# Four passes over a KV cache on one core: an even background in the last pass, weight rows on ScalarE's DMA queue, the last Wq columns transposed ahead, full PSUM units

## The chip, the core and the metric

The kernel runs as one program on one core of a Trainium2 chip. The metric is the device time of one execution in microseconds (us): the median of three runs. A hardware profile of one more execution gives the rows that are read here. The engines of the core are called TensorE (PE; its weight loads are shown apart as PEld), VectorE (DVE), ScalarE (ACT), GpSimd (POOL) and SyncE (SP); each takes its own instructions in a fixed order and waits for the others on semaphores. Sixteen DMA engines move data between device memory (HBM) and the on-chip memory (SBUF); matmuls write to PSUM.

## What is computed

One step of decoding through two equal blocks, forward and backward. Each block is attention over a cache of 65,536 positions and then a dense layer; both blocks use the same cache and the same weights:

```python
x = x + A_ref(layernorm(x), k_cache, v_cache, wq, wo)   # 32 query heads, 4 KV groups, Dh = 128
x = x + B_ref(layernorm(x), w1, b1, w2, b2)             # h = relu(ln(x) @ w1 + b1)**2 ; h @ w2 + b2
x = x + A_ref(layernorm(x), k_cache, v_cache, wq, wo)
x = x + B_ref(layernorm(x), w1, b1, w2, b2)
_out, _vjp = jax.vjp(f, x, k_cache, v_cache, wq, wo, w1, b1, w2, b2)
_grads = _vjp(grad_out)
```

One token is decoded (x is 1 x 1024, bf16), so everything is a matrix-vector product, except the gradients of the weights and of the cache, which are outer products. K and V hold 67 MB each, their gradients as much again; Wq and Wo 8.4 MB each, w1 and w2 7.3 MB each, and their gradients as much again.

## The kernel before, in words

The cache is walked four times: forward of the first block's attention (pass 1), forward of the second's (pass 2), backward of the second's (pass 3), and pass 4, which does the backward of the first's and writes the gradients of K and V for both blocks. Between the passes lie dense parts (the products with w1 and w2). The four KV groups are done one after the other. A pass is cut into **items** of 8 columns, a column being 128 positions; a group has 512 columns, so 64 items, and a pass 256. `pipeline` (L455) calls its stages item by item with a lag for each stage, and runs what stands in `bg` for that item behind them; `at` (L468) puts a task there.

**Slabs.** K and V come in slabs of 1 MB, 32 columns, four items. `Ring.slot` (L215) gives the slot that was used longest ago, and `slab` (L248) starts the transfer on SP's queue. SP takes its transfers in order: one that waits for a free slot or row buffer holds all behind it. In pass 4 the ring has the five areas 0 to 4, and area 12 until shortly before the second group; `group_done` (L1146) adds two slots after the second group and one after the third.

**Pass 4** (`attn_bwd4`, L791). Per item: `vT` transposes 8 columns of V on TensorE (L836) and `evac` (L143; ScalarE's line is L153, VectorE's L156) copies them out of PSUM; `vS` multiplies them with the gradient of the output (L855) into one PSUM tile `ps_dp`, of which there is one buffer; a matmul with `sel2` (L851) starts each such tile. When a **unit** of 24 columns is full (the last of a group has 8), VectorE multiplies it with the two blocks' exps (L864, L865) into X, GpSimd copies the exps beside them (L866, L867), and TensorE transposes X (L872). Six items behind `vT`, `k8` accumulates the gradient of the queries (L893) and forms the outer products for the gradients of K and V (L899), which VectorE and ScalarE evict as 128x1024 pieces into a staging area; after 32 columns GpSimd starts the two 1 MB writes (L906, L907). At the end of a group `dqT` is formed (L909). The unit of passes 1 to 3 is 56 columns of 64 places (`UB`, L63), the last 8.

**The background of pass 4.** `OutGrad.later` (L671) forms the output gradient of the three later groups: each of 24 rows of Wo (256 KB) is fetched into one of two buffers (L677, on SP's queue) and multiplied with a vector broadcast to all partitions, on VectorE (L381), and summed by ScalarE (L382). `outer2` (L927) makes the weights' gradients in units of 1024 output columns: two matmuls (L949), an eviction, and after two units or so a write (L953). `rows_into` (L916) lays the vectors out as rows for it: 128-column transposes (L924) and copies of 2x512 on VectorE (L925). `QueryGrad.early` (L701) multiplies rows of Wq with dqT of the first three groups, as dots on VectorE and ScalarE. Due times are written by hand (L1129 to L1144): the units for w2, w1 and Wo from item 72 to item 202, then, from item 202 to 248, the 24 dots with Wq, one an item, and the units for Wq.

**The end.** After the last group, `rows_into` for the last part of Wq's gradient, `QueryGrad.last` (L718: two slabs of Wq, a broadcast of dqT, eight row dots by `RowDots`, L385), eight units of `outer2`, the backward of the layer norm (L322) and the write of the gradient of x (L293).

**The end of pass 2.** V lags K by 76 items. When K is through, `fetch_w1` (L997) loads the eight rows of w1 for the dense part that follows into areas 6 to 13, while V goes on. Areas 10 and 11 hold the scores of the last group, from which the exps are formed (L586), areas 12 and 13 those of the group before.

The order of the instructions on each engine is not the order of these calls: the framework puts each instruction as early as its own estimate of the dependencies allows. In the built program the 24 fetches of Wo rows stand among SP's first 17 slabs of pass 4, six of them in a row, though the tasks are due over the first 170 items.

Of the kernel before, what the change touches and what calls it, by code (L numbers as in the profile page):

```python
# [18 lines left out]
def kernel(  # L19
# [42 lines left out]
    SLOTS = 512 // R  # L62
    UB = SLOTS - 8  # L63
# [3 lines left out]
    SL4 = 512 // R2  # L67
    UB4 = SL4 - 8
# [448 lines left out]
    def attn_fwd(L, order, eT, s_areas, more=None, keep=(), have=()):  # L517
# [26 lines left out]
        def kS(idx):  # L544
            g, c8 = kit[idx]
            if c8 == 0:
                state["S"] = s_areas[order.index(g) % 2].bitcast(F32).rearrange("p (r c) -> p r c", c=C)
                state["pm"] = tmp.tile([P, R, (C + UB - 1) // UB], F32, name="pm_all")
            S_sb, pm_all = state["S"], state["pm"]
            kt = state.pop(("kt", idx))  # L550
            for i in range(8):
                c = c8 + i
                slot = c % UB
                if slot == 0:
                    state["ps_s"] = ps_sc([P, SLOTS, R])
                ps_s = state["ps_s"]
                nc.tensor.matmul(ps_s[:, slot:slot + 8, :].rearrange("p a b -> p (a b)"), lhsT=kt[:, i, :],  # L557
                                 rhs=L["qpad"][:, g, :, :].rearrange("p a b -> p (a b)"), start=True, stop=True)
                if slot == UB - 1 or c == C - 1:
# [73 lines left out]
    class OutGrad:  # L633
# [37 lines left out]
        def later(self, vbc, g, bg, i0, step, rows=None, lead=None):  # L671
# [3 lines left out]
            def fetch(k):  # L675
                box[k] = rows.next()
                nc.sync.dma_start(out=box[k], in_=A_wo[g * GD + k * P:g * GD + (k + 1) * P, :])  # L677
# [16 lines left out]
    class QueryGrad:  # L694


        def __init__(self, dqT, lname):
            self.dqT, self.lname = dqT, lname
            self.y = vec.tile([P, DC, G], F32, name=lname + "_dny")

        def early(self, gs, bg, i0, step, vbc_area):  # L701
# [7 lines left out]
            def one(kc, i):  # L709
                if i == 0:  # L710
                    box["v"] = slab(w_rows(A_wq, kc * P, 1, gs[0] * GD, len(gs) * GD), 1, len(gs) * GD)
                dot_va(box["v"][:, 0, i * GD:(i + 1) * GD], box["vbc"][:, i * GD:(i + 1) * GD], self.y[:, kc, i:i + 1], GD)
            at(bg, i0, start)
            for kc in range(DC):
                for i in range(len(gs)):
                    at(bg, i0 + 1 + (kc * len(gs) + i) * step, lambda kc=kc, i=i: one(kc, i))

        def last(self, g, vbc_area):  # L718
            y = row_dots(A_wq, 0, DC, g * GD, GD, self.dqT[:, g * R:(g + 1) * R], self.lname + "_dnl", vbc_area)
            nc.vector.tensor_copy(out=self.y[:, :, G - 1], in_=y)  # L720
            dn = vec.tile([P, DC], F32, name=self.lname + "_dn")
# [3 lines left out]
    def attn_bwd3(L, og, order, eT, dqT, bg):  # L725
# [20 lines left out]
        def vS(idx):  # L746
            g, c8 = kit[idx]
            if c8 == 0:
                nc.vector.tensor_copy(out=dOpad[:, g, 0, :], in_=og.dOT[:, g * R:(g + 1) * R])
                nc.vector.tensor_copy(out=ndt[:, :, :], in_=og.nd2[:, g * R:(g + 1) * R].unsqueeze(1).to_broadcast([64, SLOTS, R]))  # L750
            vt = state.pop(("vt", idx))
            for i in range(8):
                c = c8 + i
                slot = c % UB
                if slot == 0:
                    state["ps_dp"] = ps_sc([P, SLOTS, R])
# [3 lines left out]
                last = (slot == UB - 1 or c == C - 1)  # L760
                nc.tensor.matmul(ps_dp[:, slot:slot + 8, :].rearrange("p a b -> p (a b)"), lhsT=vt[:, i, :],  # L761
                                 rhs=dOpad[:, g, :, :].rearrange("p a b -> p (a b)"), start=False, stop=last)
                if last:
                    un = slot + 1
                    c0 = c - slot
                    dsT = dst.next().rearrange("p (s r) -> p s r", r=R)
                    nc.vector.tensor_tensor(out=dsT[:, 0:un + 8, :], in0=ps_dp[:, 0:un + 8, :],
                                            in1=eT[g][:, :, c0:c0 + un + 8].rearrange("p h c -> p c h"), op=ALU.mult)
                    add_load(dve=0.07 + (un + 8) * R * 0.0019)
                    state[(g, c0 // UB)] = dsT  # L770

        def k8(idx):
# [7 lines left out]
            for i in range(8):  # L780
                c = c8 + i
                sl = c - u * UB
                nc.tensor.matmul(ps_dq[:, :, :].rearrange("p a b -> p (a b)"), lhsT=kb8[:, i, :],
                                 rhs=dsT[:, sl:sl + 8, :].rearrange("p a b -> p (a b)"), start=(c == 0), stop=(c == C - 1))
# [6 lines left out]
    def attn_bwd4(La, Lb, oga, ogb, order, eTa, eTb, dqT, bg, group_done, streams):  # L791
# [4 lines left out]
        XT = Turn([blocks(small, i) for i in range(3, 6)])  # L796
        XW = (UB4 + 1) * R4
        XS = Turn([part(small[:, 6144:], i, XW) for i in range(2)] + [part(area[5], 0, XW)])
        GGS = Turn([part(area[5][:, XW:], i, 512) for i in range(2)])
        NSL = UB4 + 4  # L800
# [345 lines left out]
    def group_done(j):  # L1146
        if j == 1:
            ring.add(e_area(1, ORD4[1]), e_area(3, ORD4[1]))
        elif j == 2:
            ring.add(e_area(1, ORD4[2]))  # L1150
# [44 lines left out]
```

## Time and profile before

| | |
|---|---|
| runs | 2063.8, 2058.95, 2060.43 us; median 2060.43 |
| profiled execution | 2060.59 us, of which span 2058.8 us |
| mean TensorE clock granted | 0.898 of full speed |
| busy share of the span: PE, PEld, DVE, ACT, POOL | 80%, 65%, 55%, 50%, 10% |
| moved | 809.62 MB, mean 393 GB/s; 640 MB read, 166 MB written |
| chain that ended last | DMA 41%, PE 31%, ACT 12%, DVE 10%, issue 5% |
| starts, from the trace | pass 2's first scores at 430 us, pass 3's at 849, pass 4's first item at 1269 |
| dqT of the last group; last issue of a DMA | 2029.8 us; 2051.25 us |

The span is from the first to the last instruction. A window row of the profile gives start and end in us, its length, then for PE, PEld, DVE, ACT and POOL the busy time and the number of instructions, the clock granted to TensorE, the mean busy share of the 16 DMA engines and the rate. A timeline row gives start, length, engine, line, operation, output and inputs, how many, and in brackets how long the engine had been idle and what released it; "SPq" is SP's queue, where the length covers several issues and their waits. A row of waits says who waited, for whom, the total in us, how often, and the longest.

### The profile page before, as it was taken

The numbers are of one execution on the slowest core, as the hardware profiler recorded it, in microseconds if no ns is written. First come the engines' busy times: TensorE is split into PE (matmuls) and PEld (weight loads), VectorE is DVE, ScalarE is ACT, GpSimd is POOL, SyncE is SP. The second block draws the span as 40 slices with busy tenths as digits, with TensorE's granted clock in tenths as the row PEclk, the third lists the DMA queues.
The fourth block names the chain that finished last, engine by engine and source line by source line (L and its number), as shares of the span: only waits on it lengthen the run. The fifth ranks groups of instructions, "written<-read, shape, count | busy, mean of one in ns | idle before, by whom it ended". The sixth has DMA issues, their size and how long they took to land.

```text
span 2058.8 us, 66212 instructions
## 1 busy us (share of the span) xinstructions
PE 1636.8 (80%) x29852; PEld 1332.2 (65%) x29852; DVE 1139.3 (55%) x1887; ACT 1037.8 (50%) x1325; POOL 200.4 (10%) x386
## 2 busy tenths in 40 slices
PE   7888886588898847788888765779888978988876
PEld 7878776578787737677777664456555545655544
DVE  4544431255444303744444557668777767768856
ACT  4543432125433302444444537768666756767855
POOL 0000000000000000000000001213222222222221
PEclk9999997579999956899999987989999999998988
DMA  9999999999999998999999997899999999998996
GB/s 381 416 417 414 412 417 407 392 358 416 414 415 414 383 392 312 345 417 414 414 417 387 401 387 309 342 347 422 401 423 417 413 424 384 424 422 339 424 423 275
DMA packets 140079, 809.62 MB, mean 393 GB/s; under 512 B 13844, under 2 KB 13844, under 8 KB 58644
## 3 DMA queue, kind: packets, MB, share of 16 engines
q1 hardware_dynamic: 112884, 639.70, 76.7%
q0 software_dynamic: 26912, 165.69, 19.7%
q8 instruction: 233, 3.82, 0.7%
q14 instruction: 50, 0.41, 0.0%
HBM read 639.64 MB, written 165.69 MB: 391 GB/s over the span
## 4 chain that ended last, share of the span: by engine, by line
DMA 41%; PE 31%; ACT 12%; DVE 10%; issue 5%; SPq 0%; POOL 0%; ACTq 0%; DVEq 0%; POOLq 0%
DMA out_dram<-pair 11%; DMA slot<-in_A_k_cache_dram 7%; DMA slot<-in_A_v_cache_dram 7%; DMA pair<-in_A_v_cache_dram 5%; PE ps_tr L539 5%; PE ps_sc L557 4%; ACT small L153 4%; DMA pair<-in_A_k_cache_dram 3%; DMA pair<-in_A_wo_dram 3%; PE ps_gg L899 3%; PE ps_acc L600 2%; PE ps_tr L836 2%; ACT pair L153 2%; PE ps_tr L741 2%; DVE pair L156 2%
## 5 line engine op out<-in xcount | busy, mean ns | idle before, releaser
L156 DVE COPY small<-ps_tr 128x1024 bf16<-128x1024 bf16 (+1 forms) x650 | 438.8, 686 | 387.5 <-PE ps_tr L539 207.5
L153 ACT COPY small<-ps_tr 128x1024 bf16<-128x1024 bf16 (+1 forms) x414 | 394.5, 967 | 431.3 <-PE ps_tr L539 248.8
L153 ACT CAST pair<-ps_gg 128x1024 bf16<-128x1024 f32 x289 | 289.9, 1015 | 144.5 <-PE ps_gg L899 100.5
L156 DVE CAST pair<-ps_gg 128x1024 bf16<-128x1024 f32 x223 | 272.3, 1221 | 105.2 <-PE ps_gg L899 79.1
L899 PE MATMUL ps_gg<-slot,small 64*128 64x512 bf16 x1024 | 202.8, 400 | 69.8 <-ACT pair L153 30.1
L557 PE MATMUL ps_sc<-L_qpad,small 128*128 128x64 bf16 x3712 | 178.4, 196 | 26.3 <-ACT small L153 14.0
L539 PE MATMUL ps_tr<-ident_b,slot 128*128 128x128 bf16 x2304 | 163.1, 224 | 15.5 <-DMA slot<-in_A_k_cache_dram 11.5
L557 PEld LDWEIGHTS <-small 128*128 128x128 bf16 x3712 | 141.8, 99 | 45.1 <-ACT small L153 25.2
L600 PE MATMUL ps_acc<-eT,slot 128*128 128x64 bf16 x2720 | 131.1, 210 | 44.9 <-DMA slot<-in_A_v_cache_dram 42.3
L539 PEld LDWEIGHTS <-slot 128*128 128x128 bf16 x2304 | 137.2, 100 | 17.5 <-DMA slot<-in_A_k_cache_dram 14.1
L600 PEld LDWEIGHTS <-slot 128*128 128x128 bf16 x2720 | 114.9, 107 | 49.4 <-DMA slot<-in_A_v_cache_dram 46.6
L899 PEld LDWEIGHTS <-small 64*128 64x128 bf16 x1024 | 58.4, 94 | 112.5 <-issue 82.1
L836 PE MATMUL ps_tr<-ident_b,slot 128*128 128x128 bf16 x1440 | 128.3, 229 | 0.4 <-DVE small L156 0.2
L539 PE MATMUL ps_tr<-ident_b,pair 128*128 128x128 bf16 x1600 | 114.3, 224 | 14.4 <-DMA pair<-in_A_k_cache_dram 13.7
L836 PEld LDWEIGHTS <-slot 128*128 128x128 bf16 x1440 | 90.8, 102 | 50.6 <-issue 46.5
L761 PE MATMUL ps_sc<-B_dOpad,small 128*128 128x64 bf16 x2048 | 101.0, 196 | 25.4 <-ACT small L153 17.6
L855 PE MATMUL ps_sc<-DOB,small 128*128 128x64 bf16 x2048 | 118.1, 198 | 0.0
L855 PEld LDWEIGHTS <-small 128*128 128x128 bf16 x2048 | 92.4, 101 | 35.9 <-issue 27.3
L539 PEld LDWEIGHTS <-pair 128*128 128x128 bf16 x1600 | 95.4, 100 | 17.4 <-DMA pair<-in_A_k_cache_dram 15.4
L761 PEld LDWEIGHTS <-small 128*128 128x128 bf16 x2048 | 78.6, 100 | 42.9 <-ACT small L153 27.2
L949 PE MATMUL ps_gg<-pair 128*128 128x512 bf16 x240 | 80.0, 412 | 27.9 <-ACT pair L153 16.1
L382 ACT ACTIVATE slot<-slot 128x1024 bf16<-128x1024 bf16 (+1 forms) x75 | 84.1, 1123 | 19.1 <-DVE slot L381 18.4
(275 smaller groups left out, 2437.6 us busy)
## 6 DMA issues: line engine op xcount, KB each, us to landing
slot<-in_A_v_cache_dram SPq DMA_DIRECT2D x164, 1024.0 KB, 17.7
slot<-in_A_k_cache_dram SPq DMA_DIRECT2D x159, 1024.0 KB, 11.8
out_dram<-pair POOLq DMA_DIRECT2D x128, 1024.0 KB, 17.8
pair<-in_A_k_cache_dram SPq DMA_DIRECT2D x82, 1024.0 KB, 19.9
pair<-in_A_v_cache_dram SPq DMA_DIRECT2D x80, 1024.0 KB, 20.0
out_dram<-eT POOLq DMA_DIRECT2D x41, 512.0 KB, 18.8
slot<-in_A_wq_dram SPq DMA_DIRECT2D x25, 768.0 KB, 11.1
slot<-in_A_wo_dram SPq DMA_DIRECT2D x16, 1024.0 KB, 12.8
```

Source lines behind the costliest of these rows:

```text
L153: nc.scalar.copy(out=out, in_=in_)
L156: nc.vector.tensor_copy(out=out, in_=in_)
L382: nc.scalar.activation(out=view, in_=view, func=ACTF.Copy, accum_out=ycol)
L539: nc.tensor.transpose(pt[:, i, :], kb8[:, i, :], ident_b[:, :])
L557: nc.tensor.matmul(ps_s[:, slot:slot + 8, :].rearrange("p a b -> p (a b)"), lhsT=kt[:, i, :], rhs=L["qpad"][:, g, :, :].rearrange("p a b - ...
L600: nc.tensor.matmul(ps_o[:, :, :].rearrange("p a b -> p (a b)"), lhsT=vb8[:, i, :], rhs=eT[g][:, :, c:c + 8], start=(c == 0), stop=(c == C ...
L741: nc.tensor.transpose(pt[:, i, :], vb8[:, i, :], ident_b[:, :])
L761: nc.tensor.matmul(ps_dp[:, slot:slot + 8, :].rearrange("p a b -> p (a b)"), lhsT=vt[:, i, :], rhs=dOpad[:, g, :, :].rearrange("p a b -> p ...
L836: nc.tensor.transpose(pt[:, i, :], vb8[:, i, :], ident_b[:, :])
L855: nc.tensor.matmul(ps_dp[:, slot:slot + 4, :].rearrange("p a b -> p (a b)"), lhsT=vt[:, i, :], rhs=DOB[:, g, :, :].rearrange("p a b -> p ( ...
L899: nc.tensor.matmul(pg[:, t2 * 512:(t2 + 1) * 512], lhsT=xt[64 * t2:64 * t2 + 64, blk0 + half, :], rhs=GG[64 * t2:64 * t2 + 64, :, :, :].re ...
L949: nc.tensor.matmul(pg[:, q0:q0 + qq], lhsT=av[:, kb + kk, :], rhs=b_rows[:, n0 + m0 + q0:n0 + m0 + q0 + qq], start=True, stop=True)
```

## The change

Four things:

1. **Units are full.** `UB` is 64 columns instead of 56, `UB4` 32 instead of 24. A column's matmul still writes up to 8 (or 4, or 2) places, but no longer past the unit's end. A group has 8 units instead of 10 in passes 1 to 3, and 16 instead of 22 in pass 4; the stage behind lags one item more. In pass 4, X has two buffers instead of three, and so has its transpose.
2. **w1 rows in pass 2** go to areas 12, 13, 10, 11, 9, 8, 7, 6, at items 1, 3, 16, 20, 24, 28, 33, 38 behind K's end, instead of 10 to 13 at 1, 3, 5, 7 and 9 to 6 at 12, 18, 24, 30.
3. **The background of pass 4.** Wo's rows are fetched on ScalarE's queue into three buffers instead of two, 8 items ahead of their due time instead of 6. `rows_into` is cut into two tasks. All units of `outer2` (w2, w1, Wq of two groups, Wo, Wq of the third) are spread evenly from item 73 to 253. The dots with Wq are in two parts: 16 for the first two groups, from item 145, each 3.5 items; 8 for the third, from item 203, each 2.5 items, with their rows fetched on ScalarE's queue into the three row buffers. `group_done` adds one slot to the ring instead of three.
4. **The last group's Wq rows** are fetched on ScalarE's queue from item 220 and transposed on TensorE from item 226 on (8 transposes and one eviction a row). Once dqT is there, 64 matmuls of one column take the place of the eight row dots.

In the built program the 24 Wo fetches, and three Wq rows behind them, stand early on ScalarE's queue as they did on SP's, but there each behind an earlier dot of ScalarE. Nearly every fetch on ScalarE waits for one earlier transfer: the framework has eight semaphores for the transfers of SP and ScalarE and gives them out in turn.

```diff
-    SLOTS = 512 // R
-    UB = SLOTS - 8
+    UB = 512 // R
-    SL4 = 512 // R2
-    UB4 = SL4 - 8
+    UB4 = 512 // R2
...
-                nc.tensor.matmul(ps_dp[:, slot:slot + 4, :].rearrange("p a b -> p (a b)"), lhsT=vt[:, i, :],
-                                 rhs=DOB[:, g, :, :].rearrange("p a b -> p (a b)"), start=False, stop=last)
+                w = min(4, UB4 - slot)
+                nc.tensor.matmul(ps_dp[:, slot:slot + w, :].rearrange("p a b -> p (a b)"), lhsT=vt[:, i, :],
+                                 rhs=DOB[:, g, 0:w, :].rearrange("p a b -> p (a b)"), start=False, stop=last)
...
-        XT = Turn([blocks(small, i) for i in range(3, 6)])
-        XW = (UB4 + 1) * R4
-        XS = Turn([part(small[:, 6144:], i, XW) for i in range(2)] + [part(area[5], 0, XW)])
+        XT = Turn([blocks(small, i) for i in (3, 4)])
+        XS = Turn([part(small, i, 1024) for i in (5, 6)])
...
-                nc.sync.dma_start(out=box[k], in_=A_wo[g * GD + k * P:g * GD + (k + 1) * P, :])
+                nc.scalar.dma_start(out=box[k], in_=A_wo[g * GD + k * P:g * GD + (k + 1) * P, :])
...
+        def fetch(self, box, kc, g, rows):
+            box[kc] = rows.next().unsqueeze(1)
+            nc.scalar.dma_start(out=box[kc][:, 0, :], in_=A_wq[kc * P:(kc + 1) * P, g * GD:(g + 1) * GD])
+
+        def transposed(self, g, bg, i0, step, areas, rows, lead):
...
+            def one(kc):
+                v = box.pop(kc)[:, 0, :]
+                pt = ps_tr()
+                for i in range(R):
+                    nc.tensor.transpose(pt[:, i, :], part(v, i, P), ident_b[:, :])
+                self.wT[kc] = blocks(areas[kc // 4], kc % 4)
+                evac(self.wT[kc], pt[:, :, :])
+            for kc in range(DC):
+                at(bg, i0 + int(kc * step) - lead, lambda kc=kc: self.fetch(box, kc, g, rows))
+                at(bg, i0 + int(kc * step), lambda kc=kc: one(kc))
+
+        def last_transposed(self, g):
+            db = tmp.tile([P, R], BF, name="dq_b")
+            nc.vector.tensor_copy(out=db[:], in_=self.dqT[:, g * R:(g + 1) * R])
+            py = ps_mv([P, DC], F32)
+            for kc in range(DC):
+                for i in range(R):
+                    nc.tensor.matmul(py[:, kc:kc + 1], lhsT=self.wT[kc][:, i, :], rhs=db[:, i:i + 1],
+                                     start=(kc == 0 and i == 0), stop=(kc == DC - 1 and i == R - 1), skip_group_check=True)
+            nc.vector.tensor_copy(out=self.y[:, :, G - 1], in_=py[:, :])
+            return self.total()
...
-        for k, i in enumerate((10, 11, 12, 13)):
-            at(bg, ik + 1 + 2 * k, lambda i=i: one(area[i]))
         at(bg, ik + 2, lambda: ring.remove(*area[6:10]))
-        for k, i in enumerate((9, 8, 7, 6)):
-            at(bg, ik + 12 + 6 * k, lambda i=i: one(area[i]))
-        at(bg, ik + 36, lambda: ring.remove(area[5]))
+        for k, i in ((1, 12), (3, 13), (16, 10), (20, 11), (24, 9), (28, 8), (33, 7), (38, 6)):
+            at(bg, ik + k, lambda i=i: one(area[i]))
+        at(bg, ik + 44, lambda: ring.remove(area[5]))
...
+    def gw_tasks():
+        yield rows_of(short_rows, [gx[:], dx2[:]], DC)
+        yield rows_of(long_rows, [L4["g"][:], L2["g"][:]], FC)
+        yield from outer2(stages, out_8, long_rows, F, short_rows, 0, D)
+        yield rows_of(short_rows, [L4["n"][:], L2["n"][:]], DC)
+        yield rows_of(long_rows, [dh4[:], dh2[:]], FC)
+        yield from outer2(stages, out_6, short_rows, D, long_rows, 0, F)
+        yield from gwq_tasks(ORD4[0:2])
+        yield rows_of(short_rows, [dx3[:], dx1[:]], DC)
+        yield rows_of(long_rows, [L3["oT"][:], L1["oT"][:]], HQ)
+        yield from outer2(stages, out_5, long_rows, QD, short_rows, 0, D)
+        yield from gwq_tasks(ORD4[2:3])
...
-        og1.later(vbx1, g, bg, IPG * j + 14, 4, wo_rows, 6)
-    LAG4 = 6
+        og1.later(vbx1, g, bg, IPG * j + 14, 4, wo_rows, 8)
+    LAG4 = 7
...
+    done = [IPG * (j + 1) + LAG4 + 1 for j in range(G)]
+    at(bg, done[0] - 12, lambda: ring.remove(area[12]))
+    at(bg, done[0], rows_ready)
+    i0, i1 = done[0] + 1, IPG * G - 3
+    tasks = list(gw_tasks())
     for t, fn in enumerate(tasks):
-        at(bg, early + t * (late - early) // len(tasks), fn)
-    qg1.early(ORD4[:-1], bg, late, 1, e_tiles[3][ORD4[2]])
-    tasks = list(gwq_tasks(ORD4[:-1]))
-    for t, fn in enumerate(tasks):
-        at(bg, late + 1 + t * (IPG * G - 8 - late) // len(tasks), fn)
+        at(bg, i0 + t * (i1 - i0) // len(tasks), fn)
+    vbcq = e_area(3, ORD4[1])
+    qg1.early(ORD4[0:2], bg, done[1] + 8, 3.5, vbcq)
+    qg1.early(ORD4[2:3], bg, done[2] + 2, 2.5, vbcq, wo_rows, 5)
+    qg1.transposed(ORD4[3], bg, done[2] + 26, 3, [e_area(1, ORD4[2]), e_area(3, ORD4[2])], wo_rows, 6)
 
     def group_done(j):
         if j == 1:
-            ring.add(e_area(1, ORD4[1]), e_area(3, ORD4[1]))
-        elif j == 2:
-            ring.add(e_area(1, ORD4[2]))
+            ring.add(e_area(1, ORD4[1]))
...
-    wq_last = gwq_tasks(ORD4[-1:])
-    next(wq_last)()
-    dn1 = qg1.last(ORD4[-1], vbx1)
-    for t in wq_last:
+    dn1 = qg1.last_transposed(ORD4[-1])
+    for t in gwq_tasks(ORD4[-1:]):
         t()
```

## The prediction

> **What bounds the kernel now.** I read the page's 40 slices first, then the table of windows of 25 us, then what the DMA queue on SP waited for, then the timelines at the places where the windows fall.
>
> ```profile
> DMA  9999999999999998999999997899999999998996
> GB/s 381 416 417 414 412 417 407 392 358 416 414 415 414 383 392 312 345 417 414 414 417 387 401 387 309 342 347 422 401 423 417 413 424 384 424 422 339 424 423 275
> ```
>
> The DMA engines are busy nearly everywhere: some 416 GB/s where the kernel only reads, 424 in the last pass, which also writes. The change moves the same 810 MB, so it can only win where the GB/s row falls: slices 14 and 15 (end of the second pass), 25 to 27 (start of the last), 37, and 40 (the end). The dips at 8, 9, 16 and 17 are the dense parts after the first and the second pass, which the change leaves alone. The windows (columns: PE, PEld, DVE, ACT, POOL busy, PE clock, DMA share, GB/s) size the dips:
>
> ```profile
> 700.00:725.00 25.00, 17.37 (x375) 15.70 (x371) 7.24 (x15) 12.73 (x25) 0.00 (x0) 0.90 0.77 310
> ...
> 1275.00:1300.00 25.00, 20.54 (x323) 14.52 (x324) 19.27 (x29) 21.63 (x30) 6.29 (x10) 1.00 0.63 230
> 1300.00:1325.00 25.00, 16.80 (x218) 10.59 (x217) 17.65 (x32) 18.04 (x24) 4.13 (x8) 0.92 0.93 362
> 1325.00:1350.00 25.00, 19.51 (x267) 13.46 (x266) 16.09 (x24) 17.24 (x24) 5.11 (x10) 0.88 0.96 363
> 1350.00:1375.00 25.00, 17.13 (x204) 11.20 (x204) 16.59 (x23) 17.77 (x24) 4.08 (x8) 0.80 0.93 361
> 1375.00:1400.00 25.00, 20.57 (x293) 13.58 (x289) 18.33 (x30) 17.26 (x20) 5.41 (x11) 0.93 0.90 359
> 1400.00:1425.00 25.00, 22.66 (x362) 15.72 (x360) 20.63 (x26) 20.79 (x23) 10.46 (x15) 1.00 1.01 421
> ...
> 1850.00:1875.00 25.00, 17.70 (x185) 12.05 (x184) 17.37 (x26) 12.36 (x17) 2.88 (x5) 0.73 0.70 290
> 1875.00:1900.00 25.00, 20.66 (x245) 13.04 (x244) 22.33 (x31) 22.34 (x33) 7.49 (x15) 0.86 0.99 383
> 1900.00:1925.00 25.00, 21.47 (x250) 13.41 (x248) 22.53 (x29) 22.68 (x32) 6.40 (x12) 0.86 1.02 425
> ...
> 2025.00:2050.00 25.00, 18.09 (x175) 10.31 (x175) 20.37 (x41) 16.33 (x21) 4.27 (x7) 0.89 0.62 249
> ```
>
> Lost DMA time is (full rate - rate) x 25 / full rate. Second pass: (416-310) x 25/416 = 6.4 us. Last pass, against 424: 11.4 in 1275:1300; 3.7, 3.6, 3.7, 3.8 in the next four, so 26.2 to 1400; 7.9 + 2.4 = 10.3 in 1850:1900; 10.3 in 2025:2050, and 8.8 us after 2050 with almost nothing moving. All windows from 1400 to 1850 together lose 10.5. The cause of each:
>
> ```profile
> 701.19 23.88 SPq L1000 DMA_DIRECT2D pair<-in_B_w_dram  x4
> ...
> 1278.25 21.86 SPq L677 DMA_DIRECT2D pair<-in_A_wo_dram  x6
> ...
> SPq L677 <- ACT pair L382: 76.7, 18, 11.7
> ...
> DVE pair L381 <- DMA pair<-in_A_wo_dram: 24.4, 10, 3.7
> ...
> 1863.74 5.01 DVE L925 CAST pair<-ps_gg 2x512 bf16<-2x512 f32 x8
> ```
>
> Twice SP's queue stands still with a row whose buffer is not free, and every slab of K and V behind it waits: four w1 rows from 701 to 725 (their areas are read by the last exps, to 724), six Wo rows from 1278 to 1300. Over the first hundred us of the last pass SP waits 76.7 us in all, 18 times, for ScalarE to finish the dot of an earlier Wo row. At 1863 eight row copies of 0.6 us stand in a row on VectorE ahead of the evictions that free everything else.
>
> **Part by part.** The sum is made against the profiled execution: 2060.59 us, span 2058.8; the median of the runs, 2060.43, is 0.2 below, so I give the two one number.
>
> *w1 rows.* The new order on SP puts two w1 rows into areas 12 and 13, whose last exps belong to the group before, and then three V slabs, ahead of the first row that needs the last exps. Before, one V slab and one such row got out. That is 3 MB more to move in the hole: 3 MB/416 = 7.2 us of work against 6.4 lost. The later 725:800 run at 401, 419, 400, so DMA bounds them and the lead is kept up to the dense part. Bounds -6.4 and 0 (the wait comes back elsewhere); I take **-6**.
>
> *Wo rows on ScalarE.* 24 issues leave SP, so a full row buffer no longer holds a slab; SP is then held only by its slots. They stay early: in the built program all 24 stand in ScalarE's first 125 or so instructions of the pass. Lost there: 26.2 us. Some stays: until the first gradient leaves at 1288 only reads can move, and at 9 us for 32 columns (outputs leave at 1288, 1297) two slabs make 2.1 MB/9 us = 233 GB/s; 12 us of that lose 12 x (424-233)/424 = 5.4. VectorE's ten waits for a row's landing (24.4 us, hence 2.4 each) may stay, with a third buffer and two items more lead against them; I keep a third, 8 us. 26.2 - 5.4 - 8 = 12.8. Added on ScalarE: 40 issues (24 Wo, 16 Wq) at SP's 0.33 us are 13 us, at POOL's 0.53 us 21, over 775 us of which ScalarE is busy 540; covered by its idle 235, and if not covered that is the price. Bounds -21 and, with the wait below, +34; I take **-13**, near the rows that have the stall.
>
> The Trainium skill, page "DMA: Bandwidth & Descriptors", section "Issuing engines are not separate DMA queues", speaks against this: started from another engine, a transfer still runs on the same 16 engines, and only the sequencer's issue time is saved. By that rule the saving would be 24 x 0.33 = 8 us at most, and the end 2035 instead of 2030. The row of 76.7 us says that what SP loses is waiting, not issuing.
>
> *Even background.* The outer-product units go from 0.73 an item (72 to 202) and then 0.55 plus 24 dots in 24 items, to 0.7 throughout; rows_into is split in two tasks. The 10.3 us at 1850 go in part: VectorE's pile of dots and eight copies is cut up, but five pairs of row tasks come where three were (1470:1485 lost about 3 so). The middle gets 16 dots (0.69 DVE, 1.15 ACT) and some 24 units: VectorE from 19 to 22.5 of 25 us. At that load 1900:1925 moves 425 GB/s, so it is carried. Bounds -10 and +5 (the dips of 1700:1750 again); I take **-6**.
>
> *Last Wq transposed ahead.* Now dqT is ready at 2029.8 and the last issue is at 2051.25; between stand rows_into, the broadcast, eight dots (transposes from 2029.3, evictions of 0.7 to 1.0 us, the last accumulate at 2046.6) and eight output evictions. After, the dots shrink to 64 matmuls of one column (224 such took 6.1 us, so 1.8) and VectorE has: 3 evictions x 1.23, 4 row copies x 0.62, 4 output evictions x 1.23, small steps 2: 13.1 us, with 2 of waits 15, against 21.4. Bounds -10 (all the dots' engine time also ahead of dqT) and -3; I take **-6**. Its eight transposes and evictions lie in the DMA-bound part.
>
> *Full units.* Per group 16 units instead of 22: 24 matmuls of L851 fewer (0.36 each, 8.6 us PE). L864/L865: 42.7 us each (84 x 0.495, 4 x 0.27) become 64 x 0.59 = 38. PE and VectorE are not the bound while the DMA share is 1.01, so **0**; if that cover went, up to -8. X has two buffers instead of three and lag 7 instead of 6, the ring loses two slots late: with five slots 1400:1475 ran at 421, so 0, at worst the +5 above.
>
> Sum: -6 - 13 - 6 - 6 = -31: 2060.6 - 31 = **2030**.
>
> **Rivals.** *The rows still pace the first group.* VectorE waits for landings as before, so nothing is won there: 2060.6 - 18 = 2043. For it: 24.4 us of waits that the issuing queue need not change. Against it: the chain of waits there runs from landing to dot to the next issue on SP, and that link is cut. The skill's rule above ends here too, if the issue time was covered.
>
> *The middle pays.* The moved background costs there what it saves at 1850: 2060.6 - 25 = 2036. Against it stands 1900:1925.
>
> *Slower: ScalarE held at its own fetches.* In the built program nearly every fetch waits for an earlier transfer, mostly a slab four or five slabs back, and behind it on ScalarE stand the evictions for which TensorE, then POOL's outputs wait. From 1275 to 1400 ScalarE is busy 92 us, with 24 issues 100. With w us held per fetch the stage lasts 100 + 24w once that exceeds 125. It eats the other 18 us at 143, so it decides from w = 1.8. At the 2.4 us that VectorE waited per row: 159, so +34 - 18 = +16: 2076. Against it: slabs that far back took some 18 us to land and were issued some eight items, over 20 us, before.
>
> *Nothing moves.* The bytes are the same and every stall comes back where DMA would have caught up: 2060. Against it: a saturated DMA cannot catch up.
>
> **Chances.** Forecast 0.58, rows still pace 0.18, the middle pays 0.10, ScalarE held 0.09, nothing 0.05. The upper bounds of all gains (6.4 + 21 + 10 + 10 = 47) give 2013; the rows case with the middle at its bound (2060.6 - 6 + 5 - 6) gives 2054. Range 2012 to 2054, with 0.86 of the chance in cases inside it, less some at their ends. About 0.2% is what a measurement can tell from no change: faster 0.86, same 0.05, slower 0.09.
>
> **What would show it.** Right: 700:725 near 415; the six-fold Wo stop gone from SP and the windows from 1300 to 1400 above 400; no window near 290 after item 200; some 15 us from dqT to the last issue. Wrong: ScalarE idle before evictions behind its fetches (slower case); L381 still waiting over 20 us for Wo rows (rows case); GB/s below 410 between items 140 and 200 (middle).

## The result, and the profile after

The changed kernel takes 2076.59 us (median; 2074.59 to 2081.16) against 2059.69 before: a ratio of 1.0081, interval 1.0059 to 1.0104. It is **slower by 17 us** where 30 us less were forecast. The profiled execution took 2081.16 us (span 2079.4), 4.6 above the median, so stages read from it add up to +20.6, not +17.

Page of the changed kernel, the row of its 40 slices:

```profile
GB/s 383 419 418 416 415 419 407 391 363 419 416 418 416 400 417 284 367 416 419 416 415 393 413 373 255 375 371 385 424 424 415 412 370 355 332 358 383 408 423 274
```

Slices 33 to 36 were at 424, 384, 424 and 422 before and are now at 370, 355, 332 and 358: a hole of 200 us where there were two short dips. The windows of 25 us of the changed kernel (columns as before the change) size it:

```profile
700.00:725.00 25.00, 15.56 (x348) 14.52 (x349) 6.66 (x13) 12.03 (x23) 0.00 (x0) 0.87 0.94 382
...
1400.00:1425.00 25.00, 23.47 (x331) 15.91 (x332) 18.82 (x26) 19.79 (x23) 8.50 (x11) 0.91 0.83 322
...
1700.00:1725.00 25.00, 14.49 (x167) 9.16 (x168) 14.05 (x18) 12.96 (x17) 3.33 (x6) 0.80 0.86 334
...
1750.00:1775.00 25.00, 20.84 (x249) 13.24 (x251) 20.48 (x32) 14.64 (x18) 4.42 (x9) 0.88 0.83 320
...
1900.00:1925.00 25.00, 18.96 (x214) 11.71 (x214) 15.61 (x21) 15.64 (x20) 4.58 (x8) 0.81 0.90 342
```

The end of pass 2 is filled better (382 for 310). The first group of pass 4 runs at 371 to 391 GB/s from 1300 to 1400, where 360 or so went before, and has a new hole at 1400. From 1700 to 1925 the engines are idler than before, VectorE busy 14 to 20 of 25 us (16 to 23 before): something waits. What VectorE waited for in pass 4 of the changed kernel (total us, times, longest):

```profile
DVE slot L379 <- DMA slot<-in_A_wq_dram: 35.1, 6, 9.4
DVE pair L379 <- DMA pair<-in_A_wo_dram: 28.1, 9, 7.2
...
DVE eT L379 <- DMA eT<-in_A_wq_dram: 9.9, 2, 6.1
DVE pair L379 <- DMA pair<-in_A_wq_dram: 5.4, 2, 5.0
DVE slot L379 <- DMA slot<-in_A_wo_dram: 3.0, 2, 2.3
```

That is 31.1 us for Wo rows and 50.4 for Wq (39.2 of them at the sixteen early dots, the rest at the third group's). Before, VectorE waited 24.4 us for Wo rows and 0.7 for Wq. One of the new waits, from the timelines of SP, of VectorE and of TensorE in the changed kernel:

```profile
1691.70 0.33 SPq L248 DMA_DIRECT2D slot<-in_A_wq_dram  x1
```

```profile
1694.14 1.22 DVE L154 CAST pair<-ps_gg 128x1024 bf16<-128x1024 f32 x1
1704.81 1.29 DVE L379 TENSOR_TENSOR slot<-slot,eT 128x1024 bf16<-128x1024 bf16 x2 [9.45 <-DMA slot<-in_A_wq_dram]
1706.02 1.22 DVE L154 CAST pair<-ps_gg 128x1024 bf16<-128x1024 f32 x1
```

```profile
1707.29 0.61 PE L938 MATMUL ps_gg<-slot,small 64*128 64x512 bf16 x2 [9.29 <-DVE pair L154]
```

SP issues the slab at 1691.7, when its slot comes free; VectorE reaches the dot at 1695.4 and stands there until 1704.8, with the evictions behind it. Without them TensorE has no PSUM and stands for 9.29 us, so it frees no slot of K or V. SP, too, stands at this slab: its next transfer but one waits until the slab has landed and then until ScalarE has summed the second dot, and goes out at 1710.0. From 1690 to 1930 TensorE and SP waited, in the changed kernel:

```profile
PE ps_gg L938 <- DVE pair L154: 33.6, 8, 9.3
...
SPq L248 <- DMA slot<-in_A_wq_dram: 22.1, 4, 9.1
SPq L248 <- ACT slot L380: 18.6, 5, 6.1
```

The first of these rows was 3.9 us before (at L899 and L156). The Trainium skill, page "PSUM — Partial Sum Buffer", section "Engine vs sequencer instructions", says that the queues of ScalarE, VectorE and GpSimd are strict FIFO. These lines agree: an eviction for which TensorE was waiting stood behind a dot that waited 9.45 us.

**A ledger by equal bytes.** Stages shift, so I summed the rate over windows of 5 us and read, for each kernel, when the same number of MB had moved. In us later than before (the kernels are those of the experiments; the last row compares spans of the profiled executions):

| MB moved | changed | b_w1 | b_rows | a_gwo | a_nodot | a_best |
|---|---|---|---|---|---|---|
| 280, pass 2 nearly through | -3.0 | -0.1 | +0.4 | -4.4 | -3.0 | -4.9 |
| 320, dense part | -8.2 | -5.0 | +0.7 | -9.7 | -8.1 | -9.9 |
| 500, pass 3 nearly through | -8.6 | -4.6 | +0.3 | -10.3 | -8.5 | -12.3 |
| 580, first group of pass 4 through | -4.5 | -3.4 | +15.6 | -20.5 | -8.1 | -19.8 |
| 660 | -5.7 | -4.6 | +16.1 | -17.6 | -9.0 | -20.2 |
| 740 | +22.2 | -3.7 | +14.9 | +3.6 | -11.4 | -16.4 |
| 780 | +20.5 | -3.0 | +15.4 | +2.5 | -12.6 | -24.3 |
| end | +20.6 | -3.2 | +15.4 | -0.2 | -16.1 | -26.1 |

So the changed kernel wins 3.0 in pass 1 and 2 and 5.2 at the w1 rows, loses 4.1 in the first group and **27.9 between 660 and 740 MB**, and the rest is level.

### The profile page after: what moved, and what is told of

The parts are those of the page before. It is cut to its first block, busy times and chain, and to the rows that moved or that the text cites. A ratio compares the mean times of both kernels' runs of the same rounds, so it can differ in the third digit from the quotient of the medians.

```text
span 2079.4 us, 65988 instructions
## 1 busy us (share of the span) xinstructions
PE 1620.9 (78%) x29819; PEld 1332.6 (64%) x29884; DVE 1124.8 (54%) x1815; ACT 1026.0 (49%) x1277; POOL 187.8 (9%) x334
## 4 chain that ended last, share of the span: by engine, by line
DMA 40%; PE 32%; DVE 11%; ACT 11%; issue 5%; POOL 0%; another core or an unknown queue 0%; SPq 0%; ACTq 0%; DVEq 0%; POOLq 0%
DMA out_dram<-pair 7%; DMA slot<-in_A_k_cache_dram 7%; DMA slot<-in_A_v_cache_dram 6%; DMA pair<-in_A_k_cache_dram 5%; PE ps_tr L537 4%; ACT small L151 4%; DMA slot<-in_A_wq_dram 4%; PE ps_tr L781 4%; PE ps_gg L938 3%; DMA pair<-in_A_wo_dram 3%; PE ps_sc L556 3%; PE ps_tr L875 3%; DVE pair L154 2%; DVE small L154 2%; DMA pair<-in_A_v_cache_dram 2%
## 5 line engine op out<-in xcount | busy, mean ns | idle before, releaser
L154 DVE COPY small<-ps_tr 128x1024 bf16<-128x1024 bf16 x658 | 443.7, 687 | 342.9 <-PE ps_tr L537 172.6
L151 ACT COPY small<-ps_tr 128x1024 bf16<-128x1024 bf16 x382 | 382.1, 1014 | 430.4 <-PE ps_tr L537 232.9
L938 PE MATMUL ps_gg<-slot,small 64*128 64x512 bf16 x1024 | 203.3, 405 | 98.6 <-DVE pair L154 70.2
L556 PE MATMUL ps_sc<-L_qpad,small 128*128 128x64 bf16 (+7 forms) x3712 | 172.6, 193 | 25.5 <-ACT small L151 12.1
L537 PE MATMUL ps_tr<-ident_b,slot 128*128 128x128 bf16 x2304 | 163.5, 224 | 15.3 <-DMA slot<-in_A_k_cache_dram 13.3
L938 PEld LDWEIGHTS <-small 64*128 64x128 bf16 x1024 | 60.9, 94 | 145.9 <-issue 112.2
L875 PE MATMUL ps_tr<-ident_b,slot 128*128 128x128 bf16 x1600 | 150.9, 228 | 3.6 <-DVE small L154 1.7
L537 PEld LDWEIGHTS <-slot 128*128 128x128 bf16 x2304 | 137.3, 100 | 17.9 <-DMA slot<-in_A_k_cache_dram 16.2
L599 PEld LDWEIGHTS <-slot 128*128 128x128 bf16 x2720 | 115.2, 107 | 43.0 <-DMA slot<-in_A_v_cache_dram 40.5
L875 PEld LDWEIGHTS <-slot 128*128 128x128 bf16 x1600 | 101.5, 101 | 54.8 <-issue 48.3
L537 PE MATMUL ps_tr<-ident_b,pair 128*128 128x128 bf16 x1600 | 113.9, 223 | 12.6 <-DMA pair<-in_A_k_cache_dram 12.5
L895 PE MATMUL ps_sc<-DOB,small 128*128 128x64 bf16 (+3 forms) x2048 | 120.2, 197 | 0.8 <-issue 0.2
L802 PE MATMUL ps_sc<-B_dOpad,small 128*128 128x64 bf16 (+7 forms) x2048 | 102.5, 195 | 23.3 <-ACT small L151 16.3
L932 PE MATMUL ps_acc<-small,slot 128*128 128x64 bf16 (+1 forms) x1920 | 110.5, 198 | 0.6
L537 PEld LDWEIGHTS <-pair 128*128 128x128 bf16 x1600 | 95.1, 100 | 15.0 <-DMA pair<-in_A_k_cache_dram 14.3
## 6 DMA issues: line engine op xcount, KB each, us to landing
slot<-in_A_k_cache_dram SPq DMA_DIRECT2D x167, 1024.0 KB, 12.3
out_dram<-pair POOLq DMA_DIRECT2D x128, 1024.0 KB, 14.3
out_dram<-eT POOLq DMA_DIRECT2D x44, 512.0 KB, 14.8
```

Source lines behind the costliest of these rows:

```text
L151: nc.scalar.copy(out=out, in_=in_)
L154: nc.vector.tensor_copy(out=out, in_=in_)
L537: nc.tensor.transpose(pt[:, i, :], kb8[:, i, :], ident_b[:, :])
L556: nc.tensor.matmul(ps_s[:, slot:slot + w, :].rearrange("p a b -> p (a b)"), lhsT=kt[:, i, :], rhs=L["qpad"][:, g, 0:w, :].rearrange("p a b ...
L599: nc.tensor.matmul(ps_o[:, :, :].rearrange("p a b -> p (a b)"), lhsT=vb8[:, i, :], rhs=eT[g][:, :, c:c + 8], start=(c == 0), stop=(c == C ...
L802: nc.tensor.matmul(ps_dp[:, slot:slot + w, :].rearrange("p a b -> p (a b)"), lhsT=vt[:, i, :], rhs=dOpad[:, g, 0:w, :].rearrange("p a b -> ...
```

## The experiments

Labels beginning with b start from the kernel before, those with a from the changed one. All were timed against the kernel before, whose median was 2059.8 to 2060.9 each time.

**The parts alone.** b_w1 has the new order of w1 rows only (the diff of part 2). b_rows moves only the Wo fetch:

```diff
-                nc.sync.dma_start(out=box[k], in_=A_wo[g * GD + k * P:g * GD + (k + 1) * P, :])
+                nc.scalar.dma_start(out=box[k], in_=A_wo[g * GD + k * P:g * GD + (k + 1) * P, :])
```

> The kernel before with one part of the change alone, the new order of the w1 rows. By equal bytes moved, the changed kernel gains 5.1 us between 280 and 300 MB, where the four w1 rows held the queue on SP. If the order of the rows did that, this kernel is 5 to 6 us faster than before (2054 to 2055 for 2059.7) and its window 700:725 moves over 370 GB/s. If the gain came from elsewhere in the change (the full units of the second pass), it is within 1 us of before.

Measured: 2056.91 us, ratio 0.9979 (0.9970 to 0.9989); 700:725 moves 383 GB/s. The order of the rows is worth 4 to 5 us, where 5 to 6 were expected. Its -0.1 at 280 MB, where the table's kernels with full units have -3.0 to -4.9, shows that the full units are worth some 3 us or more in pass 1 and 2.

> The kernel before with one part of the change alone: the 24 Wo rows are issued by ScalarE instead of SP (two row buffers, lead of six items, as before). If the queue was what held the first group, as the prediction's term of 13 us has it, 2045 to 2050. If the rows' landing on VectorE paces the first group whoever issues them (the rival that the rows still pace it), 2056 to 2064, with VectorE waiting over 20 us for Wo rows. If ScalarE as the issuer adds its own delay, as the changed kernel with its rows on SP suggests (2069 against 2077), 2064 to 2070.

Measured: **2074.61 us**, ratio 1.0074 (1.0059 to 1.0089), worse than the worst that was expected. All of it arises between 500 and 580 MB. VectorE's wait for Wo rows in b_rows, and one case of it from the timelines of ScalarE and of VectorE:

```profile
DVE pair L381 <- DMA pair<-in_A_wo_dram: 38.6, 13, 7.6
```

```profile
1358.35 0.19 ACT L382 ACTIVATION_READ_ACCUMULATOR pair<-pair 128x1 f32 x1
1358.45 0.79 ACT L153 COPY small<-ps_tr 128x768 bf16<-128x768 bf16 x1
1360.61 1.01 ACT L153 CAST pair<-ps_gg 128x1024 bf16<-128x1024 f32 x1 [1.38 <-PE ps_gg L899]
...
1366.18 1.79 ACTq L677 DMA_DIRECT2D pair<-in_A_wo_dram  x2
```

```profile
1376.72 0.69 DVE L381 TENSOR_TENSOR pair<-pair 128x1024 bf16<-128x1024 bf16 x1 [7.55 <-DMA pair<-in_A_wo_dram]
```

The row's buffer is free at 1358.5, but its fetch stands behind five evictions and a dot on ScalarE, some of which wait for TensorE; it goes out at 1366.2, has landed at 1376.7, and VectorE has stood for 7.55 us. Over all 22 fetches that reuse a buffer, the time from the end of the dot that frees it to the issue is 2.4 us on average (up to 7.6); on SP before it was 0.05 (median 0.03). ScalarE is not held by its fetches: among its waits from 1262 to 1440 there is none for a transfer. Its fetches are held by ScalarE, and the chain from dot to buffer to issue to landing to dot, which paces the group, gets longer. A full round of it takes 14.4 us on average, against 9.7 before. Of the 4.7 us more, 2.4 lie before the issue, 0.6 between the issue and VectorE's part of the dot, and 1.7 between that and the end of ScalarE's part. So the later issue is half of it; the other half arises as ScalarE and VectorE get to the dot later.

**The queue in the changed kernel.** a_sync puts both kinds of rows back on SP:

```diff
-                nc.scalar.dma_start(out=box[k], in_=A_wo[...
+                nc.sync.dma_start(out=box[k], in_=A_wo[...
-            nc.scalar.dma_start(out=box[kc][:, 0, :], in_=A_wq[...
+            nc.sync.dma_start(out=box[kc][:, 0, :], in_=A_wq[...
```

> The changed kernel with the Wo and Wq rows back on SP's queue. If ScalarE is held at its own fetches (the slower rival of the prediction), this is faster than the changed kernel by 10 us or more. By the landing theory the queue matters little by itself: SP is held again by rows whose buffer is not free (three buffers now), VectorE waits as long for their landing, and the time lies between 2076 and 2090.

Measured: 2069.39, ratio 1.0045 (1.0027 to 1.0063): 7 us faster than the changed kernel, between the two expectations and in neither. SP is held by Wo rows again (51.0 + 11.9 us), yet VectorE waits 17.6 us for them instead of 31.1. In this order of dots, SP is the better issuer, though the two intervals just overlap.

**Dots held to their items.** As built, all 24 Wo dots stand on VectorE within the first 44 items. A dot is held by rewriting a column of its broadcast vector from that item's X, unchanged in value:

```diff
+    cur = {}
+
+    def gate(vbc):
+        nc.vector.scalar_tensor_tensor(out=vbc[:, 0:1], in0=cur["X"][:, 0, 0:1], scalar=0.0, in1=vbc[:, 0:1],
+                                       op0=ALU.mult, op1=ALU.add)
...
+                if rows is not None:
+                    gate(vbc)
                 dot_va(view, vbc, self.dOT[:, g * R + k:g * R + k + 1], D)
...
+                    cur["X"] = X
```

> The changed kernel with its 24 Wo dots held to their items in the same way (the fetches keep a lead of eight items in the program); as built, all 24 stand on VectorE within the first 44 of 256 items. Theory (landing): VectorE's 31 us of waits for Wo rows and the hole of 8 us at 1400:1425 go, sixteen of the dots leave the first group, and the time falls by 8 to 13 us, to 2064 to 2069. Rival (ScalarE's queue): the fetches stay on ScalarE, so nothing changes, 2076.6. Rival (the first group is short of work for the DMA anyway, the first results being late): under 3 us.

Measured: 2064.28, ratio 1.0016 (1.0006 to 1.0025), 12 us under the changed kernel, as the landing theory had it. VectorE has no wait for a Wo row left. Two windows of a_gwo:

```profile
1300.00:1325.00 25.00, 21.52 (x338) 14.96 (x338) 21.47 (x29) 20.99 (x25) 7.15 (x12) 1.00 1.01 414
...
1400.00:1425.00 25.00, 20.02 (x310) 13.73 (x311) 18.51 (x28) 16.86 (x18) 5.93 (x11) 1.00 1.01 424
```

The first group runs at 414 GB/s or more from 1300 on; at 580 MB the kernel is 16 us ahead of the changed one. Only eight of the 24 dots are left in the first group, so the run does not separate the waits that are gone from the sixteen dots that are. The middle's loss stays (+21 between 660 and 740).

> The changed kernel with the sixteen early Wq dots of the first two groups changed in two ways: each Wq slab is fetched eight items before its dot, and the dot cannot be placed earlier than its item, since it reads a column that a small VectorE operation on that item's X has just rewritten. Theory (landing): from 1690 to 1930 VectorE stands 46 us in front of Wq dots whose rows have not landed, with all evictions behind it, and this is what costs the changed kernel 28 us between 660 and 740 MB; then the waits fall under 10 us, the windows from 1700 to 1925 return above 400 GB/s and the time to 2050 to 2057. Rival (ring): the ring has two slots fewer there than before and takes 8 slabs of Wq besides, so slabs come too late whoever waits; a slab fetched earlier holds its slot longer, and the time stays within 5 us of 2076.6 or grows. Rival (ScalarE's queue holds its own evictions): no change, 2076.6.

Measured: 2064.69, ratio 1.0020 (1.0011 to 1.0029), outside all expectations, and it separates nothing: at eight items ahead the ring, which does not hold these slabs, hands their slot to a later slab before the dots, so the dots run on that slab and change it. They then waited for TensorE's reads instead (18.7 us).

**The Wq dots.** a_nodot keeps the eight slabs and leaves out the dots:

```diff
-                dot_va(box["v"][:, 0, i * GD:(i + 1) * GD], box["vbc"][...
+                if not skip:
+                    dot_va(box["v"][:, 0, i * GD:(i + 1) * GD], box["vbc"][...
...
```

> The changed kernel with the sixteen early Wq dots left out (the gradient of the first input lacks their part); the 8 Wq slabs are still fetched into the ring at the same places on SP. Theory (VectorE stands in front of the landing, 50 us of waits, and holds the evictions that free everything else): 2050 to 2057, the windows from 1700 to 1925 above 400 GB/s. Rival (the 8 slabs take slots and queue places from K and V, whoever waits): 2066 to 2077, and the dips between 1700 and 1925 stay.

Measured: **2047.90**, ratio 0.9934 (0.9919 to 0.9948): 29 us under the changed kernel and 2 under what was expected. A window of a_nodot:

```profile
1750.00:1775.00 25.00, 21.52 (x250) 13.71 (x252) 17.51 (x21) 18.15 (x19) 6.13 (x11) 0.93 1.01 423
```

Not all windows come back: of the nine from 1700 to 1925 four stay under 400 GB/s (362 to 397), against seven in the changed kernel. The slabs take the same slots and the same places on SP, and the loss from 660 to 740 MB turns into a gain of 2.4 us. SP even stands longer for them to land, 64.4 us from 1690 to 1930 against 29.2. So slabs of Wq in the ring are not by themselves what cost the time; the dots on them were. Two things go with the dots, and the run does not separate them: VectorE's waits, with the evictions behind them, and the 23.8 us for which SP, after the landing, waited for ScalarE to finish the dots. Their own work, 16 x 0.69 us on VectorE and 16 x 1.15 on ScalarE, goes too; but a_best below, which has the dots, wins 4.1 us from 660 to 780 MB, and this kernel 3.6.

**Own buffers for the Wq rows.** a_wqrows fetches them as 256 KB rows into five buffers, eight items ahead; a_wqrows_g holds their dots as well. The third and the last group's rows use the five buffers too.

```diff
...
-    qg1.early(ORD4[0:2], bg, done[1] + 8, 3.5, vbcq)
+    spare = e_area(3, ORD4[1])[:, 2048:4096]
+    wq_rows = Turn(wo_rows.areas + [part(spare, i, 1024) for i in range(2)])
+    qg1.early(ORD4[0:2], bg, done[1] + 8, 3.5, vbcq, wq_rows, 8)
...
```

> The changed kernel with the sixteen early Wq dots fed by rows of 1024 through five row buffers of their own (the three of Wo and two in the unused half of the broadcast area) on ScalarE's queue, eight items ahead in the program, instead of slabs in the ring. The ring then carries K and V alone. Nothing holds a dot back to its item. Rival (ring too short): the 8 slabs are gone from the ring, so the windows from 1700 to 1925 return above 400 GB/s and the time falls to 2050 to 2057 even though nothing holds the dots. Landing theory: the dots still stand on VectorE ahead of rows that have not landed; VectorE waits over 20 us for Wq and the time stays between 2066 and 2080.

> The same, with each early Wq dot held to its item by a small VectorE operation that reads that item's X and rewrites one column of the broadcast vector. Landing theory: VectorE's waits for Wq fall under 10 us and the time is 2048 to 2057. Ring rival: no better than the same kernel without the hold. If both need to be right, this one gains and the one without the hold gains about half.

Measured: 2044.62 (ratio 0.9926, 0.9898 to 0.9955) and 2046.08 (0.9931, 0.9909 to 0.9952). In both, Wq rows overwrite some of the last group's Wo rows ahead of their dots, so the output gradient of that group is another. Here my theory, as put, fell: nothing holds the dots in a_wqrows, and still VectorE's waits for Wq go from 50.4 to 21.0 us and the time by 32 us. The hold adds nothing: with it VectorE waits 29.5 us for Wq, where under 10 were expected, and the time is the same. For the Wq dots it is not the place of the dot that counts. What does, the early fetch, the buffers of their own or the ring that carries K and V alone, these two runs do not separate. By themselves they would have spoken for the ring; a_nodot, where the slabs stay in the ring, speaks against a ring that is too short for the slabs, and leaves open what SP's waits behind the dots cost.

**All together.** a_best has the Wq rows so, all dots held, and the Wo dots of the second and third later group at items 68 and 102, so that no buffer is shared:

```diff
...
-    for j, g in enumerate(ORD4[1:]):
-        og1.later(vbx1, g, bg, IPG * j + 14, 4, wo_rows, 8)
+    for g, i, step in ((ORD4[1], 14, 4), (ORD4[2], IPG + 4, 4), (ORD4[3], IPG + 38, 4)):
+        og1.later(vbx1, g, bg, i, step, wo_rows, 8)
...
```

> All dots held: Wq as in the kernel above and the 24 Wo dots too, those of the second and third group moved to items 68 to 96 and 102 to 130, so that the row buffers are free when the Wq rows begin. Landing theory: the 12 us that holding the Wo dots gave and the 20 to 28 us of the Wq dots add up: 2076.6 - 12 - 24 = 2040, between 2034 and 2048. Ring rival or a bound by the work of VectorE and ScalarE in the middle: 2055 or more.

Measured: **2036.03**, ratio 0.9884 (0.9863 to 0.9906), faster than both kernels and within what was expected. Its four windows from 1300 to 1400 move 411 to 424 GB/s, and those from 1750 to 1925 404 to 424; 1700:1750 stays at 371 and 391.

> The same as the kernel with all dots held (2036), with nothing holding any dot to its item: five row buffers for Wq, Wo rows of the second and third group earlier in the program. If the hold is what brings the Wo dots' gain, the waits for Wo return (over 15 us) and this takes 2043 to 2049; if the buffers and the order in the program do it, 2034 to 2038.

a_best_n drops `gate` everywhere. Measured: 2050.00, ratio 0.9948 (0.9928 to 0.9967), a little above the range for the hold; VectorE waits 34.1 us for Wo again.

> The kernel with all dots held (2036), with the hold taken from the Wq dots and kept on the Wo dots. In the two kernels that differ by the hold of the Wq dots alone so far (2044.6 without, 2046.1 with), it brought nothing: then 2033 to 2038. If the Wq dots crowd forward as the Wo dots did, 2040 to 2048, with waits for Wq over 20 us.

a_best_wo drops it for Wq alone. Measured: 2039.53, ratio 0.9898 (0.9882 to 0.9915): between its two ranges, not told apart from a_best. VectorE waits 30.1 us for Wq (a_best 16.1), as the second case had it. Of the 14 us of a_best_n some 10 are the Wo dots'.

> The kernel with all dots held (2036), its Wo and Wq rows issued by SP instead of ScalarE. If holding the dots is all that counts, 2034 to 2040. If a row whose buffer is not yet free holds the slabs behind it on SP, 2042 to 2052, with SP waiting over 20 us for row buffers.

a_best_sync exchanges `nc.scalar.dma_start` for `nc.sync.dma_start` for the rows. Measured: 2042.50, ratio 0.9917 (0.9902 to 0.9931). That is the case in which a row without a buffer holds the slabs: SP waits for row buffers 14.8 us in the first group and some 109 in all of pass 4. With held dots ScalarE is the better issuer by 6 us, though the two intervals just touch, where SP was with crowded dots.

> The kernel before with the new order of the w1 rows, and its Wo rows fetched on ScalarE's queue with their dots held to their items; the background, the tail and the units stay as before. Landing theory: 4 us from the w1 rows and about 12 to 13 us from the first group (what the changed kernel with held Wo dots gained there against before), less some 4 us for sixteen dots that move into the later groups: 2060.9 - 4 - 12 + 4 = 2049, between 2042 and 2053. If the gain of holding needs the third buffer or the even background, 2055 to 2060.

b_best is b_rows with the w1 order and `gate`. Measured: 2046.72, ratio 0.9932 (0.9916 to 0.9947), as the landing theory had it. Holding 24 dots turns the +15 of b_rows into about -10 (the w1 order has 4 of the 14 us that are won), with two buffers and the old background.

**The end.** a_tail puts the layer norm's chain ahead of the output units; a_best_last takes the old end:

```diff
...
-    dn1 = qg1.last_transposed(ORD4[-1])
+    dn1 = qg1.last(ORD4[-1], vbx1)
...
```

> The same as the kernel with all dots held (2036), with the end reordered: the chain that ends in the last small output is placed ahead of the output matmuls of the last group, behind which its TensorE step stood for 7 us (it ended the program in both kernels before this). If that place was the end, 2029 to 2032; if the two-buffer cycle of the last eight output evictions sets the end as well, between 2034 and 2037, since they only move behind it.

Measured: 2040.91, ratio 0.9902 (0.9888 to 0.9917): slower than expected. The outputs' last issue comes 24.5 us after dqT, against 21.4 in a_best, since they now stand behind the chain. That dqT itself comes 3.6 us later is not explained.

> The same as the kernel with all dots held (2036), with the end as before the change: the last group's Wq dots after the last gradient of q, nothing transposed ahead. If the transposed form is worth the 6 us of the prediction, 2041 to 2043; if it is worth the 1 to 2 us that the changed kernel's trace shows from 780 MB to its end, 2036 to 2038.

Measured: 2040.01, ratio 0.9892 (0.9875 to 0.9909). From dqT to the last issue it takes 28.4 us, a_best 22.6. So the transposed form saves 5.8 us of the end in the traces, of which the times show some 4, not clear of noise. Not all of it is the form's: here the second slab of Wq is issued at 1984.2 and lands at 2006.9, 4 us after dqT, and TensorE stands 3.0 us for it. In the kernel before both slabs were issued over 30 us ahead of dqT, and the same end took 21.4 us.

## Why the prediction was wrong, step by step

- **w1 rows, -6:** right; -5.2 by bytes, and -4.0 in time for the order alone (b_w1).
- **Wo rows on ScalarE, -13:** the wrong sign; +4 in the changed kernel, +15 alone. The step that failed is "SP is then held only by its slots": true, but the group was paced by the rows' own chain, and I let 12.8 us go with SP's stop. The rival that rows still pace it named the chain, but cut its link on SP and overlooked that ScalarE's link is longer (2.4 us against 0.05). Its sign came: VectorE still waits 31.1 us for Wo rows. The slower rival's price of 2.4 us a fetch and its 2076 come close to what was measured by chance: it had the evictions wait behind the fetch, while the fetch waited behind the evictions, and in the changed kernel most of the loss lies elsewhere. The Trainium skill's rule that the prediction cites (page "DMA: Bandwidth & Descriptors", section "Issuing engines are not separate DMA queues"), that issuing from several engines only saves the sequencer's time, allowed 8 us at most. None were won: b_rows shows that an issue can also come later.
- **Even background, -6:** the largest miss, +26 from 660 to 780 MB. "At that load 1900:1925 moves 425 GB/s, so it is carried" counted the dots' busy time and not their landing. In that window of the kernel before, the slabs had landed when VectorE came to their dots. There the dots wait for the broadcast: the first three slabs go out at 1820, 1836 and 1841, and the first dot runs at 1858 without a wait. Spread out, each slab is fetched when a slot comes free and its dot is next on VectorE, which stood 39.2 us at the sixteen dots. Taking the dots out took the loss away (a_nodot); whether the evictions behind VectorE's waits or SP's waits behind the dots cost more stays open. The rival that the middle pays had the place right, and its sign came, but it priced the middle at nothing won. In a_best, where rows are early and have their own buffers, the same spread is nearly carried: it loses 3.8 us between 660 and 740 MB, and wins 7.9 between 740 and 780.
- **Last Wq transposed, -6:** the dots did shrink to 1.9 us, and a_best_last and a_best differ by 5.8, a late slab included; but against the kernel before nothing is won: 21.2 us from dqT to the last issue, forecast 15. The term was mis-sized, above all in the output evictions. From the timeline of the changed kernel, dqT, the dots, the first output eviction and the last issue:

```profile
2050.94 0.15 DVE L948 SCALAR_TENSOR_TENSOR B_dqT<-ps_acc,L_rZ 128x8 f32<-128x8 f32 x1
...
2056.41 1.85 PE L755 MATMUL ps_gg<-dq_b,eT 128*128 128x1 bf16 x64 [0.83 <-DVE pair L154]
...
2062.12 1.23 DVE L154 CAST eT<-ps_gg 128x1024 bf16<-128x1024 f32 x1 [0.34 <-PE ps_gg L988]
...
2072.13 0.31 SPq L291 DMA_DIRECT2D out_dram<-ctd_rows  x1
```

  From dqT to the dots it takes 5.5 us of evictions (I had 3.7), the dots 1.9, and the eight output evictions, from 2062.1 to 2070.4, 8.3 us where I had 4.9 by VectorE's half: two PSUM buffers pass between TensorE and either engine, and each waits for the round. Before, the eight output evictions ran from 2040.1 to 2049.8 with the row dots between them. TensorE's granted clock was 0.50 from 2056 to 2066 in the changed kernel, and 0.76 to 0.90 in the stretches of 5 us from 2035 to 2050 before; what part of the 8.3 us is due to that is not shown.
- **Full units, 0:** -3.0 in pass 1 and 2, inside the bound of -8; the prediction worked it out for pass 4 alone.

Sum by bytes: -3.0 - 5.2 - 0.4 + 4.1 - 1.2 + 26.2 + 0.1 = +20.6, for a forecast of -31.

## What to carry to other kernels

Work that reads a fresh transfer and sits in an in-order engine with the evictions has to be costed by when its data lands, not by its busy time: find the issue, add the landing, and see what stands behind it. Moving a fetch to another queue moves it behind that engine's work, and which queue was better turned with the place of the dots: SP where they crowd forward, ScalarE where they are held. Two things won most here: fetching Wq rows ahead into buffers of their own, 32 us, and holding the early-placed Wo dots back to their turn, 12 us in the changed kernel. Holding the Wq dots won nothing that these runs can tell from noise.

## What was not expected of the hardware

- A fetch goes out a mean of 0.05 us after its buffer is free on SP (before) and of 2.4 us on a ScalarE that also evicts (b_rows). A Wo row then lands after 5.8 us in the median, up to 10.9, in the seven landings that the trace of b_rows gives; in the four of before the median is 7.7.
- From 2050 to 2075 in the changed kernel TensorE's granted clock was 0.63, with TensorE busy 14.3 us of 25, and 0.50 from 2054 to 2065. A matmul of L938 took 0.58 to 0.61 us from 2053.3 on, and 0.38 to 0.39 at 2030.7.
